# Expert output also kept unsplit in SBUF, activation sums formed there, one more pass by seven products

## The chip, the cores and the metric

The kernel runs on one core of a Trainium2 chip. The metric is the device time of one execution in microseconds (us); several executions are timed and their median is given. One execution more is recorded by the hardware profiler.

The engines are TensorE (PE in the views; PEld is its weight load), VectorE (DVE), ScalarE (ACT), GpSimd (POOL) and SyncE (SP), which issues most DMA transfers. Each works through its own list of instructions in order and waits for the others by semaphores. SBUF is the memory beside the engines, PSUM the memory that TensorE writes.

## The reference

Bucketed attention over 2 x 8 heads of 768 tokens gives x (1536 tokens x 512). A router sends each token to one of 8 experts. Then a gated layer follows, with `d_ff` of 1536:

```
for e in range(E):
    mask = e_idx == e
    h = np.maximum(x[mask] @ w1[e], 0.0)
    out[mask] = gate_w[mask, None] * eom[mask, e, None] * (h @ w2[e])
...
a = x @ w_a
b = x @ w_b
return (a * b @ w_out).astype(np.float32)
```

## The kernel before, in words

**Precision.** Every product is made of three: an operand is split into a rounded high part (suffix `h`, type F32R) and the rest (`l`), and high times high, low times high and high times low are added in PSUM. The high part is a ScalarE copy into F32R, the low part a subtraction on VectorE or GpSimd.

**Stages.** Attention comes first; its program is untouched. Then the expert stage (from about 260 us): 8 experts in 8 steps each. A step multiplies the tokens of an expert by a piece of w1 (`mm1`), takes the result out of PSUM as `hl` (high part on ScalarE, low part on VectorE), and multiplies the `hl` of the step before by a piece of w2 (`mm2`). `y_sum` and `y_store` take an expert's result out in the first two steps of the next expert: `y_store` writes the high part `y_h` on ScalarE and the low part `y_l` on VectorE, at a column that is read from a register (the count of tokens ahead of the expert). `y_evac` does it for the last expert. Tokens are thus columns 0 to 1535 of `y_h` and `y_l`; the four rows of 128 features are the index `d`.

**Second layer** (from 436 us). The columns are two tiles of 768 (`c` = 0 and 1), the 1536 features of the layer are 12 chunks of 128 (`f`). A pass is one chunk for one tile; here it is called f0c0, f0c1, f1c0, f1c1, f2c0 and so on, which is also the order in time. A pass makes a and b for its 768 tokens and multiplies them, in two halves of 384 tokens. There are two ways:

- `ab`: for each half 2 x 4 x 3 products of 384 columns, 48 a pass. The a bank is copied out by ScalarE (L1068), VectorE multiplies it by the b bank (L1069), `rounded` splits the result into `gh` (ScalarE) and `gl` (VectorE, queued after the next half's product).
- `seven`: Strassen's scheme in Winograd's form over two halves of the tokens and two halves of the features, 7 x 2 x 3 = 42 products a pass. It needs sums of weights (`s1` to `s4`, `s_work`) and sums of activations (t1 to t4, `t_work`), both split again. Its first product is copied out as p1 (L1185), the sum u2 adds p1 to the second, and the third adds to the first's bank, so it waits until p1 has been copied; the fourth (`s3`) adds to the second's bank and waits for u2.

Before, f0 and f1 go by `ab` for both tiles, and f2 to f11 by `seven`. The activation sums are made in these four passes from `y_h + y_l` in a buffer `accs`, which later holds the accumulators of 9 of the 12 output blocks (the other three keep a PSUM bank each):

```
t1, t2, t3, t4 = TF = [af[:, o:o + 768].rearrange("p (a b) -> p a b", a=2) for o in at]
...
whole(t3, lo_d, b), whole(t1, lo_d, a), tt(t1, t3, t1), whole(t2, hi_d, b), tt(t3, t2, t3),
tt(t2, t2, t1), tt(t4, yh[:, hi_d, a], t2), tt(t4, t4, yl[:, hi_d, a], ALU.add), hi(1),
```

**Side work.** Between the products stand fill units (`outp`: three matmuls of 512 columns that multiply `gh`, `gl` by the output weights; every second unit is followed by scaling its bank on ScalarE or VectorE) and the conversion of later weights. These arrive as 64-bit floats in pieces of 512 KB (`r2`, loaded by `w2_load` in the order of `SEQ`). A conversion is a chain over two engines: `w2_a` (t, ScalarE), `w2_s` (flags, VectorE), `w2_k` (x, ScalarE, which also issues the next load), `w2_b` (the shift b, VectorE). `w2_c` splits a piece of output weights (h2 on ScalarE, l2 on GpSimd), `part` one of the weights or weight sums into a `pc` (high part on ScalarE, low part on GpSimd). `todo_of` says at which of seven steps of a pass each is issued, `units` which fill units it has, and the loop at the end (L1247 to L1283) emits the passes. The order of every engine is the order in which the code emits.

In the `ab` passes steps 0 to 2 come behind the first half's matmuls and steps 3 to 6 behind the second's; in `seven`, step k comes behind product k.

Of the kernel before, what the change touches and what calls it, by code (L numbers as in the profile page):

```python
# [23 lines left out]
C = 224  # L24
# [9 lines left out]
def attn_moe_kernel(ctx: ExitStack, tc: tile.TileContext, xin, cst, projd, wblk, wmoe, w2in, out):  # L34
# [567 lines left out]
    with tc.manual_schedule():  # L602
# [209 lines left out]
        for y in (y_h, y_l):  # L812
# [4 lines left out]
        s2 = ctx_2.enter_context(tc.tile_pool(name="s2", bufs=3, reuse_waits="tile"))  # L817
# [23 lines left out]
        def w2_a(*k):  # L841
            T2[k] = c2.tile([128, 512], F32, tag="t2", name="t2", bufs=5)
            f64_hi(R2[k], T2[k])

        def w2_s(*k):
            X2[k] = c2.tile([128, 512], U32, tag="x2", name="x2")
            DVE.tensor_scalar(out=X2[k], in0=T2[k].bitcast(U32), scalar1=0x80000000, scalar2=None, op0=ALU.bitwise_and)

        def w2_k(*k):
# [5 lines left out]
            w2_load(SEQ.index(k) + 3)  # L855
# [15 lines left out]
        SW = {}  # L871
# [5 lines left out]

        def part(m, nm):
            src = SW[nm] if nm in SW else a_part(m, nm)
            p = s2.tile([128, 2, 256], F32R, tag="pc", name="pc", bufs=9)  # L880
# [103 lines left out]
        def cc_work():  # L984
# [20 lines left out]
            (7, 7): [ids_load],  # L1005
# [3 lines left out]
        for n, (e, f) in enumerate(steps):  # L1009
# [13 lines left out]
            if e == E - 4 and f in (2, 4, 6):  # L1023
# [19 lines left out]
        accs = fast.tile([128, 9, 512], F32, name="accs")  # L1043
        af = accs.rearrange("p a b -> p (a b)")
# [13 lines left out]
        def ab(c, f, hf):  # L1058
# [8 lines left out]
            a = tmp(("c11", "c21")[hf])  # L1067
# [6 lines left out]
        def outp(k, f):  # L1074
# [36 lines left out]
        def t_work(c):  # L1111
            yh, yl = y_h.bitcast(F32), y_l.bitcast(F32)
            at = ((3072, 0, 768, 1536), (2304, 0, 768, 1536))[c]
            t1, t2, t3, t4 = TF = [af[:, o:o + 768].rearrange("p (a b) -> p a b", a=2) for o in at]

            def whole(o, d, n):
                return lambda: DVE.tensor_tensor(out=o, in0=yh[:, d, n], in1=yl[:, d, n], op=ALU.add)

            def tt(o, x, y, op=ALU.subtract):
                return lambda: DVE.tensor_tensor(out=o, in0=x, in1=y, op=op)  # L1120

            def hi(i):
                return lambda: ACT.activation(TH[c][i], TF[i], ACTF.Copy)

            def low(i):
                th = TH[c][i].bitcast(F32) if i else yh[:, lo_d, n2[c]]
                return lambda: DVE.tensor_tensor(out=TL[c][i], in0=TF[i], in1=th, op=ALU.subtract)

            a, b = n1[c], n2[c]
            return [  # L1130
                whole(t3, lo_d, b), whole(t1, lo_d, a), tt(t1, t3, t1), whole(t2, hi_d, b), tt(t3, t2, t3),
                tt(t2, t2, t1), tt(t4, yh[:, hi_d, a], t2), tt(t4, t4, yl[:, hi_d, a], ALU.add), hi(1),
                hi(2), low(1), hi(3), low(2), low(3),
            ], [hi(0), low(0)]

        def s_work(m, k):
            def new(nm):
                SW[nm] = fast.tile([128, 256], F32, tag=nm, name=nm)
                return SW[nm]

            if k == 0:
                DVE.tensor_tensor(out=new("s1"), in0=a_part(m, "21"), in1=a_part(m, "22"), op=ALU.add)
                DVE.tensor_tensor(out=new("s2"), in0=SW["s1"], in1=a_part(m, "11"), op=ALU.subtract)
            elif k == 1:
                DVE.tensor_tensor(out=new("s3"), in0=a_part(m, "11"), in1=a_part(m, "21"), op=ALU.subtract)
            else:
                DVE.tensor_tensor(out=new("s4"), in0=a_part(m, "12"), in1=SW["s2"], op=ALU.subtract)

# [14 lines left out]
        def seven(c, m, fill, side, low):  # L1163
# [40 lines left out]
            c21 = add(tmp("c21"), y, p1)  # L1204
# [139 lines left out]
```

## Time and profile before

| | |
|---|---|
| median of 3 runs | 741.96 us (741.78 to 743.85) |
| the profiled execution | 742.49 us |
| its span, first to last instruction | 740.7 us |
| mean granted TensorE clock | 0.992 of 2.4 GHz |
| TensorE busy, matmuls | 715.0 us (97%), 4561 |
| VectorE busy | 554.2 us (75%), 1099 instructions |
| ScalarE busy | 439.6 us (59%), 929 |
| GpSimd busy | 223.0 us (30%), 261 |
| bytes moved by DMA | 88.48 MB, mean 119 GB/s |

Matmuls overlap at their ends, so the busy time of TensorE is no measure of how densely they follow each other; the start of one to the start of the next is. An engine that shows no idle time in a stretch may still be late for another. In the rows of the timelines the bracket at the end tells how long the engine had been idle and which instruction, by engine, tile and line, released it. Times in rows are from the span's start. The granted clock is a share of 2.4 GHz; TensorE has two levels, 1.2 and 2.4.

### The profile page before, as it was taken

To read this page: it belongs to the slowest core of one execution; us is meant where nothing else is said; L and a number is where in the kernel's file an instruction comes from. 1 tells how busy PE (TensorE), PEld (TensorE's weight loads), DVE (VectorE), ACT (ScalarE), POOL (GpSimd) and SP (SyncE) were. 2 spreads that over 40 slices of the span, in tenths; PEclk is the share of its full clock that TensorE was granted. 3 is DMA by queue.
4 is the path that set the end of the run, shared out by engine and by line. 5 is a ranking of instruction groups with operands and counts; after the bars stand their busy time and mean duration, and the time that the engine had idled before them with its cause. 6 is when DMAs were issued, how large, how long until landed. Compare 5 with 4: busy or idle time off the path is not lost.

```text
span 740.7 us, 13120 instructions
## 1 busy us (share of the span) xinstructions
PE 715.0 (97%) x4561; PEld 612.0 (83%) x4562; DVE 554.2 (75%) x1099; ACT 439.6 (59%) x929; POOL 223.0 (30%) x261
## 2 busy tenths in 40 slices
PE   8899999999999999999999998799999999999995
PEld 6676777776776789999999997788999999999994
DVE  6778777888776678777778858866777777777653
ACT  6878777777777357666677745456443453434311
POOL 3233232333533283212210002133223332233215
PEclk9999999999999999999999999899999999999998
DMA  7357351321301068888898612121212212120003
GB/s 239 118 214 262 102 167 58 105 69 66 134 8 60 15 223 241 241 188 243 267 238 275 209 30 85 38 78 57 86 35 80 86 58 86 33 81 31 1 30 145
DMA packets 42681, 88.48 MB, mean 119 GB/s; under 512 B 7328, under 2 KB 10736, under 8 KB 42608
## 3 DMA queue, kind: packets, MB, share of 16 engines
q1 hardware_dynamic: 39936, 81.07, 35.5%
q0 software_dynamic: 2304, 6.31, 2.3%
q8 instruction: 38, 0.62, 0.4%
q14 instruction: 35, 0.29, 0.1%
q10 hardware_dynamic: 368, 0.20, 0.1%
HBM read 73.32 MB, written 13.12 MB: 117 GB/s over the span
## 4 chain that ended last, share of the span: by engine, by line
PE 79%; DVE 7%; issue 6%; ACT 3%; POOL 3%; DMA 2%; SPq 0%; POOLq 0%; ACTq 0%; DVEq 0%
PE tp L186 9%; PE av L201 8%; PE y L951 6%; PE s L158 4%; PE s L159 4%; PE h L913 4%; PE h L912 3%; PE h L911 3%; PE y L952 3%; PE aba L1156 3%; PE abb L1156 3%; PE aba L1158 3%; PE aba L1157 3%; PE abb L1158 3%; PE abb L1157 3%
## 5 line engine op out<-in xcount | busy, mean ns | idle before, releaser
L164 DVE TENSOR_REDUCE mm<-s 128x1 f32<-128x768 f32 x96 | 91.1, 949 | 25.1 <-PE s L159 24.1
L173 ACT ACTIVATE p<-s,sb 128x768 f32<-128x768 f32 x96 | 94.8, 988 | 21.7 <-DVE sb L165 21.0
L186 PEld LDWEIGHTS tp<-cs,p 128*128 128x128 f32 x576 | 64.2, 140 | 36.7 <-ACT p L173 23.4
L485 DVE TENSOR_TENSOR wl<-wr,wh 128x512 fp32r<-128x512 f32 x125 | 81.5, 692 | 8.4 <-ACT wh L484 3.1
L186 PE MATMUL tp<-cs,p 128*128 128x128 f32 x576 | 82.2, 279 | 4.8 <-ACT p L173 3.9
L190 ACT ACTIVATE pt<-tp 128x384 f32<-128x384 f32 x143 | 64.9, 487 | 32.6 <-PE tp L186 32.6
L484 ACT ACTIVATE wh<-wr 128x512 fp32r<-128x512 f32 x128 | 73.7, 623 | 3.2 <-DMA wr<-wmoe 3.0
L951 PE MATMUL y<-hl,wh 128*128 128x448 f32 x224 | 74.8, 377 | 0.1
L158 PE MATMUL s<-tk,tq 76*128 76x384 f32 x192 | 73.1, 381 | 0.3 <-DVE tq L135 0.3
L911 PE MATMUL h<-xh,wh 128*128 128x224 f32 x256 | 71.5, 279 | 0.2 <-ACT xh L418 0.2
L913 PE MATMUL h<-xh,wl 128*128 128x224 f32 x256 | 70.7, 276 | 0.2 <-DVE wl L485 0.2
L912 PE MATMUL h<-xl,wh 128*128 128x224 f32 x256 | 70.3, 274 | 0.3 <-DVE xl L419 0.3
L882 POOL TENSOR_TENSOR pc<-t,pc 128x256 fp32r<-128x256 f32 x38 | 30.0, 791 | 128.8 <-ACT pc L881 59.8
L201 PE MATMUL av<-pt,v 128*64 128x384 f32 x360 | 68.0, 499 | 0.2 <-DVE r L225 0.2
L1052 ACT ACTIVATE gh<-c 128x384 fp32r<-128x384 f32 x28 | 14.7, 526 | 88.2 <-DVE c L1175 67.8
L159 PE MATMUL s<-bk,bq 128*128 128x384 f32 x192 | 65.1, 339 | 0.0
L952 PE MATMUL y<-hl,wl 128*128 128x224 f32 x224 | 59.6, 266 | 0.0
L911 PEld LDWEIGHTS h<-xh,wh 128*128 128x128 f32 x256 | 49.0, 191 | 1.3 <-ACT xh L418 0.4
L913 PEld LDWEIGHTS h<-xh,wl 128*128 128x128 f32 x256 | 49.2, 192 | 0.4 <-DVE wl L485 0.4
L912 PEld LDWEIGHTS h<-xl,wh 128*128 128x128 f32 x256 | 49.2, 192 | 0.5 <-DVE xl L419 0.5
L201 PEld LDWEIGHTS av<-pt,v 128*64 128x64 f32 x360 | 21.9, 136 | 32.7 <-issue 24.5
L882 POOL TENSOR_TENSOR pc<-s,pc 128x256 fp32r<-128x256 f32 x40 | 36.0, 910 | 42.8 <-ACT pc L881 42.8
(235 smaller groups left out, 1921.9 us busy)
## 6 DMA issues: line engine op xcount, KB each, us to landing
wr<-wmoe SPq DMA_DIRECT2D x128, 256.0 KB
r<-w2in SPq DMA_DIRECT2D x36, 512.0 KB
x<-xin SPq DMA_DIRECT2D x30, 384.0 KB
xr<-zero SPq DMA_DIRECT2D x13, 512.0 KB
xg<-xr SPq DMA_DIRECT2D x14, 256.0 KB
v<-xin SPq DMA_DIRECT2D x16, 192.0 KB
wb<-wblk SPq DMA_DIRECT2D x1, 640.0 KB
x<-xin SPq DMA_DIRECT2D x3, 192.0 KB
```

The lines of the kernel that those rows point to most:

```text
L158: PE.matmul(p[:, c, :384], T[h, 0][:76, qs], T[h, 1][:76, sl], start=True, stop=False)
L159: PE.matmul(p[:, c, :384], B[h, 0][:, qs], B[h, 1][:, sl], start=False, stop=True)
L164: DVE.tensor_reduce(out=m[:, 1:2], in_=st[g][:, :, :384], axis=AX.XY, op=ALU.min)
L173: ACT.activation(p.rearrange("p (c n) -> p c n", c=2), st.pop(g)[:, :, :384], ACTF.Exp, scale=scl.pop(g), bias=nbs.pop(g), accum_out=sums[ ...
L186: PE.transpose(ps[:, j * 128:(j + 1) * 128], pt_[g][:, k * 128:(k + 1) * 128], ident)
L201: PE.matmul(av[h][c * 64:(c + 1) * 64, :384], v, PT[h][:, k, c * 384:(c + 1) * 384], start=(k == 0), stop=(k == NT - 1), skip_group_check= ...
L485: eng.tensor_tensor(out=l, in0=r, in1=h.bitcast(F32), op=ALU.subtract)
L911: PE.matmul(ps, wh, xh, start=first, stop=False)
L912: PE.matmul(ps, wh, xl, start=False, stop=False)
L913: PE.matmul(ps, wl, xh, start=False, stop=last)
L951: PE.matmul(p, wh[:, w], hl, start=(f == 0), stop=False, skip_group_check=True)
L952: PE.matmul(p[:, 0], wl[:, w], hl[:, 0], start=False, stop=(f == 7), skip_group_check=True)
```

## The change

The expert result is stored a third time, unsplit, as `y_w` (128 x 4 x 1760, F32): `y_store` gets four ScalarE copies more, the last expert two, and `y_w` is cleared by four memsets on GpSimd. `t_work` makes t1 to t4 in place in `y_w`, by four subtractions per tile instead of eight operations. The columns of `y_w` then hold the nine accumulators; `accs` is gone. Pass f1c0 goes by `seven`, f1c1 stays with `ab`. So the sums of tile 0 have to be ready by f1c0, and so have the weight sums of chunk 1, which are new: `s_work(1)` stands in the last two steps of the expert stage, and eight pieces of chunk 1 (the seven of `seven` and 21, which f1c1 needs) instead of four are made in f0c0 and f0c1. The conversion of (2,1) moves from f0c1 to f1c1. To make room, `r2` has 2 buffers instead of 3 (a load is issued two pieces ahead, not three), `t2` 4 instead of 5, `x2` 1 instead of 2; `h2`, `l2` and five of nine `pc` buffers lie in a pool that reuses the expert stage's memory.

The diff, cut (moved but unchanged functions are left out):

```diff
+        y_w = yp.tile([128, 4, N + C], F32, name="y_w")
+        for y in (y_h.bitcast(F32), y_l.bitcast(F32), y_w):
             for d in range(4):
-                POOL.memset(y.bitcast(F32)[:, d], 0.0)
-        r2 = ctx_2.enter_context(tc.tile_pool(name="r2", bufs=3, reuse_waits="tile"))
+                POOL.memset(y[:, d], 0.0)
+        r2 = ctx_2.enter_context(tc.tile_pool(name="r2", bufs=2, reuse_waits="tile"))
...
-        SEQ = [(0, 0), (0, 1), (1, 0), (1, 1), (0, 2)]
-        for m in range(2, 12):
+        SEQ = [(0, 0), (0, 1), (1, 0), (1, 1), (0, 2), (2, 0), (1, 2), (2, 1)]
+        for m in range(3, 12):
...
-            w2_load(SEQ.index(k) + 3)
+            w2_load(SEQ.index(k) + 2)
...
+        def pc_tile(shape, dt, nm):
+            pcs[0] += 1
+            return (s2 if (pcs[0] - 1) % 9 < 4 else fast).tile(shape, dt, tag="pc", name=nm, bufs=4 if (pcs[0] - 1) % 9 < 4 else 5)
...
         def y_store(e):
             sl = bass.ds(o_regs[e], C)
             for d in range(4):
-                y = YS.pop((e, d))
+                y = YS[e, d]
                 ACT.activation(y_h[:, d, sl], y, ACTF.Copy)
                 DVE.tensor_tensor(out=y_l[:, d, sl], in0=y, in1=y_h.bitcast(F32)[:, d, sl], op=ALU.subtract)
+            for d in range(4):
+                ACT.activation(y_w[:, d, sl], YS.pop((e, d)), ACTF.Copy)
...
+            (7, 6): [lambda: s_work(1, 0)],
+            (7, 7): [ids_load, lambda: s_work(1, 1), lambda: s_work(1, 2)],
...
-            if e == E - 4 and f in (2, 4, 6):
+            if e == E - 4 and f in (2, 4):
                 w2_load(f // 2 - 1)
...
         for i in range(2):
             y_evac(E - 1, i)
+        for i in range(2):
+            src = Y[E - 1][i].rearrange("p (a b) -> p a b", a=2)[:, :, :C]
+            ACT.activation(y_w[:, 2 * i:2 * i + 2, bass.ds(o_regs[E - 1], C)], src, ACTF.Copy)
...
-            o = accs[:, (k - 6) % 9]
+            if not own:
+                d, at = AT[k - 3]
+                o = y_w[:, d, at:at + 512]
...
+            a, b = n1[c], n2[c]
+            w = (y_w[:, lo_d, a], y_w[:, hi_d, b], y_w[:, lo_d, b], y_w[:, hi_d, a])
...
+                tt(w[0], w[2], w[0]), tt(w[2], w[1], w[2]), tt(w[1], w[1], w[0]), tt(w[3], w[3], w[1])
+            ] + [g(i) for i in (1, 2, 3, 0) for g in (hi, low)]
...
+            if (c, f) == (0, 0):
+                for k, g in zip((0, 0, 0, 1, 3, 3, 4, 5, 6, 6), t):
+                    m[k].append(g)
+                conv(0, 2, 1, 1, 1, 2)
+                put(4, w2_c, 0)
+                for k, nm in ((2, "11"), (3, "s2"), (4, "12"), (5, "s3"), (6, "s1")):
+                    put(k, part, 1, nm)
+            elif (c, f) == (1, 0):
+                t = t_work(0)
+                put(0, t[10])
+                put(1, t[11])
+                conv(2, 0, 2, 2, 2, 3)
+                put(4, cc_work)
+                for k, nm in ((4, "22"), (5, "s4"), (6, "21")):
+                    put(k, part, 1, nm)
+            elif (c, f) == (0, 1):
+                t = t_work(1)
+                for k in range(4):
+                    put(k, t[k])
+                conv(1, 2, 3, 4, 4, 5)
+                put(6, w2_c, 1)
+            elif (c, f) == (1, 1):
+                conv(2, 1, 0, 0, 0, 1)
+                for k, g in zip((1, 1, 2, 3, 3, 4), t[4:10]):
+                    m[k].append(g)
+                for k in range(3):
+                    put(2 + k // 2, s_work, 2, k)
+                conv(3, 0, 4, 4, 4, 5)
+                conv(3, 1, 5, 5, 5, 6)
+                for k, nm in ((0, "11"), (1, "12"), (2, "s2"), (3, "s3"), (3, "s1"), (4, "22"), (5, "s4")):
+                    put(k, part, 2, nm)
+                put(6, t[10])
+                put(6, t[11])
...
-                if f < 2:
+                if f < 2 and (c or not f):
                     for hf in range(2):
+                        if (c, f, hf) == (0, 0, 0):
+                            for g in work[0]:
+                                g()
+                            work[0] = []
                         last, low = low, ab(c, f, hf)
```

How the order moves, at two places. VectorE, from the first product c of f0c0 on (c_6176 before; the first and second half's product are c_6176 and c_6219), before:

```order
L1069 TENSOR_TENSOR c_6176<-abb,c_6176 128x384
L1117 TENSOR_TENSOR accs<-y_h,y_l 128x768
L847 TENSOR_SCALAR x_6185<-t_6182 128x512
L1117 TENSOR_TENSOR accs<-y_h,y_l 128x768
L859 SCALAR_TENSOR_TENSOR t_6182<-t_6182,x_6185 128x512
L1120 TENSOR_TENSOR accs<-accs 128x768
L1069 TENSOR_TENSOR c_6219<-abb,c_6219 128x384
L1054 TENSOR_TENSOR gl<-c_6176,gh 128x384
L1117 TENSOR_TENSOR accs<-y_h,y_l 128x768
L1120 TENSOR_TENSOR accs<-accs 128x768 x2
L1120 TENSOR_TENSOR accs<-y_h,accs 128x768
```

and now, where the second half's product writes p_6263 and the shifted weights are t_6226:

```order
L1142 TENSOR_TENSOR y_w<-y_w 128x2x384 x3
L1093 TENSOR_TENSOR c_6219<-abb,c_6219 128x384
L1142 TENSOR_TENSOR y_w<-y_w 128x2x384
L848 TENSOR_SCALAR x_6228<-t_6226 128x512
L860 SCALAR_TENSOR_TENSOR t_6226<-t_6226,x_6228 128x512
L1093 TENSOR_TENSOR p_6263<-abb,p_6263 128x384
L1078 TENSOR_TENSOR gl<-c_6219,gh 128x384
L1142 TENSOR_TENSOR tl_6184<-y_w,th_6178 128x768
L1142 TENSOR_TENSOR tl_6185<-y_w,th_6179 128x768
L1142 TENSOR_TENSOR tl_6186<-y_w,th_6180 128x768
```

Three of the four sums stand ahead of the first product, the additions of y_h and y_l are gone, and the three low parts of tile 0 stand in the second half of f0c0.

ScalarE in f1c1, from the split of the second half's product (c_6536, `gh`) to the copy p1 of f2c0 (p_6587); q are the banks that are scaled into the accumulators, t and x the conversion, before:

```order
L1052 ACTIVATE gh<-c_6536 128x384
L1096 ACTIVATE accs<-q_6499,cc 128x512
L850 ACTIVATE x_6547<-r_6326 128x512
L881 ACTIVATE pc<-s_6434 128x256
L881 ACTIVATE pc<-s_6430 128x256
L1123 ACTIVATE th_6143<-accs 128x768
L1096 ACTIVATE accs<-q_6556,cc 128x512
L881 ACTIVATE pc<-t_6284 128x256
L881 ACTIVATE pc<-s_6437 128x256
L1123 ACTIVATE y_h<-accs 128x2x384
L1185 ACTIVATE p_6587<-aba 128x384
```

and now, where the split and one scaled bank stand ahead of these rows, and p_6631 is p1:

```order
L1145 ACTIVATE th_6183<-y_w 128x768
L900 ACTIVATE pc<-s_6538 128x256
L900 ACTIVATE pc<-s_6534 128x256
L496 ACTIVATE t_6595<-r_6442 128x512
L851 ACTIVATE x_6597<-r_6442 128x512
L900 ACTIVATE pc<-t_6509 128x256
L1122 ACTIVATE y_w<-q_6590,cc 128x512
L496 ACTIVATE t_6610<-r_6514 128x512
L851 ACTIVATE x_6612<-r_6514 128x512
L900 ACTIVATE pc<-s_6582 128x256
L1145 ACTIVATE y_h<-y_w 128x2x384
L1191 ACTIVATE p_6631<-abb 128x384
```

Two conversions (t_6595 and t_6610, each with its x) stand behind the third high part, where there was none; the third, of (2,1), stands further ahead in the same pass, as the two of before do (the x of the second is in the rows).

## Rows read from the trace of the kernel before

**Rows 1.** TensorE timeline 452 to 496: start us, us, engine, line, operation, [idle before <- releaser].
```profile
457.29 0.45 PE L911 MATMUL aba<-y_h,pc 128*128 128x384 f32 x1 [3.06 <-ACT c L1068]
...
477.29 0.79 PE L1087 MATMUL q<-h,gl 128*128 128x512 f32 x1 [3.78 <-DVE gl L1054]
...
491.57 0.44 PE L1156 MATMUL aba<-y_h,pc 128*128 128x384 f32 x1 [0.57 <-ACT p L1185]
...
494.50 0.44 PE L1156 MATMUL abb<-th,pc 128*128 128x384 f32 x1 [0.92 <-DVE u L1171]
```

**Rows 2.** Windows: stretch, us, busy of PE, PEld, DVE, ACT, POOL, granted clock, DMA share, GB/s.
```profile
473.50:476.60 3.10, 0.01 (x1) 0.00 (x0) 3.07 (x5) 0.00 (x0) 0.00 (x0) 0.99 0.01 3
476.60:483.40 6.80, 6.11 (x18) 5.73 (x19) 2.54 (x5) 5.49 (x11) 2.49 (x3) 0.50 0.25 78
```

**Rows 3.** TensorE timeline, 483.7 to 485.5; eight matmuls are left out.
```profile
483.70 0.34 PE L911 MATMUL abb<-y_h,pc 128*128 128x384 f32 x1
...
485.27 0.39 PE L1085 MATMUL q<-h,gh 128*128 128x512 f32 x1
485.50 0.40 PE L1086 MATMUL q<-l,gh 128*128 128x512 f32 x1
```

**Rows 4.** VectorE and GpSimd timelines of pass f1c1.
```profile
475.35 0.95 DVE L1127 TENSOR_TENSOR y_l<-accs,y_h 128x768 fp32r<-128x768 f32 x1
476.22 0.55 DVE L1069 TENSOR_TENSOR c<-abb,c 128x384 f32<-128x384 f32 x1
...
478.02 0.42 DVE L847 TENSOR_SCALAR x<-t 128x512 uint32<-128x512 uint32 x1
...
490.06 1.49 DVE L1127 TENSOR_TENSOR tl<-accs,th 128x768 fp32r<-128x768 f32 x1
...
481.53 0.74 POOL L882 TENSOR_TENSOR pc<-t,pc 128x256 fp32r<-128x256 f32 x1 [0.61 <-PE aba L913]
```

**Rows 5.** Expert stage: ScalarE and TensorE timelines around 331 and 421.
```profile
330.90 1.22 ACT L975 ACTIVATE y_h<-yt 128x224 f32 x4
332.28 0.36 ACT L924 ACTIVATE hl<-h 128x224 fp32r<-128x224 f32 x1 [0.16 <-PE h L913]
...
334.63 0.38 PE L951 MATMUL y<-hl,wh 128*128 128x448 f32 x1
...
420.93 0.33 ACT L924 ACTIVATE hl<-h 128x224 fp32r<-128x224 f32 x1
...
422.01 0.27 PE L940 MATMUL y<-hl,wh 128*128 128x224 f32 x1
422.27 0.37 PE L943 MATMUL y<-hl,wh 128*128 128x224 f32 x1
```

**Rows 6.** Windows, as group 2: the 2.2 us in which one 512 KB load moves.
```profile
507.40:509.60 2.20, 2.20 (x13) 2.06 (x13) 1.41 (x3) 1.70 (x4) 1.35 (x2) 1.00 0.75 235
```

**Rows 7.** TensorE and VectorE timelines at the end of f0c0.
```profile
444.86 0.34 PE L911 MATMUL aba<-y_h,pc 128*128 128x384 f32 x1
...
445.39 0.55 DVE L1069 TENSOR_TENSOR c<-abb,c 128x384 f32<-128x384 f32 x1
```

**Rows 8.** ScalarE timeline of pass f1c1, one row of each kind.
```profile
476.81 0.52 ACT L1052 ACTIVATE gh<-c 128x384 fp32r<-128x384 f32 x1 [5.81 <-DVE c L1069]
477.24 0.67 ACT L496 ACTIVATE t<-r 128x512 f32<-128x512 f32 x1
477.80 0.41 ACT L881 ACTIVATE pc<-t 128x256 fp32r<-128x256 f32 x1
478.18 0.69 ACT L1096 ACTIVATE accs<-q,cc 128x512 f32<-128x512 f32 x1
478.77 0.77 ACT L850 ACTIVATE x<-r 128x512 uint8<-128x512 uint8 x1
...
479.70 0.83 ACT L1123 ACTIVATE th<-accs 128x768 fp32r<-128x768 f32 x1
...
491.03 0.48 ACT L1185 ACTIVATE p<-aba 128x384 f32<-128x384 f32 x1
```

More of the change, by code (lines that the diff above doesn't have):

```diff
@@ L876, in a_part, with s_work, new @@
             return T2[m, i][:, o:o + 256]
+        def s_work(m, k):
+            def new(nm):
+                SW[nm] = s2.tile([128, 256], F32, tag=nm, name=nm, bufs=1)
+                return SW[nm]
+            if k == 0:
+                DVE.tensor_tensor(out=new("s1"), in0=a_part(m, "21"), in1=a_part(m, "22"), op=ALU.add)
+                DVE.tensor_tensor(out=new("s2"), in0=SW["s1"], in1=a_part(m, "11"), op=ALU.subtract)
+            elif k == 1:
+                DVE.tensor_tensor(out=new("s3"), in0=a_part(m, "11"), in1=a_part(m, "21"), op=ALU.subtract)
+            else:
+                DVE.tensor_tensor(out=new("s4"), in0=a_part(m, "12"), in1=SW["s2"], op=ALU.subtract)
         def part(m, nm):
             src = SW[nm] if nm in SW else a_part(m, nm)
-            p = s2.tile([128, 2, 256], F32R, tag="pc", name="pc", bufs=9)
+            p = pc_tile([128, 2, 256], F32R, "pc")
             ACT.activation(p[:, 0], src, ACTF.Copy)
@@ L1041, in attn_moe_kernel @@
         G = {}
-        accs = fast.tile([128, 9, 512], F32, name="accs")
-        af = accs.rearrange("p a b -> p (a b)")
+        AT = ((0, 0), (1, 0), (2, 0), (3, 0), (2, 1024), (3, 1024), (0, 1024), (1, 1024), (2, 512))
         def tmp(nm):
@@ L1129, in t_work @@
-            a, b = n1[c], n2[c]
+                th = TH[c][i].bitcast(F32) if i else y_h.bitcast(F32)[:, lo_d, b]
+                return tt(TL[c][i], w[i], th)
             return [
[L1131 to L1147, printed above, removed]
+                tt(w[0], w[2], w[0]), tt(w[2], w[1], w[2]), tt(w[1], w[1], w[0]), tt(w[3], w[3], w[1])
+            ] + [g(i) for i in (1, 2, 3, 0) for g in (hi, low)]
@@ L1228, in todo_of, with conv, put @@
-            if c == 0:
-                m[3].append(lambda: w2_c(f))
+            m = [[] for _ in range(7)]
+            def conv(n, i, *at):
+                for k, g in zip(at, (w2_a, w2_s, w2_k, w2_b)):
+                    m[k].append(lambda g=g: g(n, i))
+            def put(k, g, *a):
+                m[k].append(lambda: g(*a))
+            if f < 2:
+                t = t_work(c)
+            if (c, f) == (0, 0):
[31 more added lines that the diff above has]
+                put(6, t[11])
+            elif c == 0:
+                conv(f, 2, 0, 1, 1, 2)
+                put(3, w2_c, f)
+                if f < 11:
+                    for k, at in ((0, 4), (1, 4), (2, 5)):
+                        put(at, s_work, f + 1, k)
@@ L1230, in todo_of @@
             elif f < 11:
-                for k, nm in enumerate(ORDER if f else ("11", "12", "21", "22")):
-                    m[k].append(lambda nm=nm: part(f + 1, nm))
+                for i in range(2 * (f < 10)):
+                    conv(f + 2, i, *((0, 1, 1, 2), (3, 4, 4, 5))[i])
+                for k, nm in enumerate(ORDER):
+                    put(k, part, f + 1, nm)
             return m
@@ L1242, in units @@
             return [(k, i) for k in range(3) for i in (f - 2, f - 1) if i >= 0]
-        ts = [t_work(c) for c in range(2)]
-        todo = ts[0][0] + ts[1][0]
         low = None
```

51 lines of the change are left out of this document (12 added, 39 removed).

## Prediction

> **What bounds the kernel now.** TensorE is busy for 97% of the span, so I looked first for the stretch where it isn't. The view by slices sends the reader to 450 to 500 us, the first passes of the second layer; TensorE's own timeline there shows who is waited for [rows 1]. Pass f1c0 starts 3.06 late because ScalarE had not copied the half ahead of it out of PSUM; the fill matmuls of f1c1 stand still for 3.78 behind a VectorE subtraction; f2c0 waits 0.57 for the copy p1 and 0.92 for the sum u2. The windows show a second price of the 3.78: work stopped at 473.5, the granted clock went from 0.99 to 0.50 at 476.6, that is from 2.4 to 1.2 GHz, and stayed there for 6.8 us [rows 2]. 6.1 us of that were under work, so about 3 us were lost (2.8 by the matmuls in it). The 3.06 wait left no such mark. After 494.5 TensorE streams matmuls to the end, so a gain before that point reaches the end whole, through the last products and the row scatters behind them.
>
> So the sum is a race over one stretch, from the first product of f0c0, near 436, to 494.50 (product s3 of f2c0). All times below are on the clock of the profiled execution: 742.49 us, of which 740.7 are the span; the median of the runs, 741.96, is 0.53 lower.
>
> **What leaves.** A matmul of 384 columns costs TensorE 0.175 (nine from 483.70 to 485.27), one of 512 columns 0.23 [rows 3]. f1c0 by seven products has 42 instead of 48: 1.05 us less. The sums t1 to t4 lose per tile three additions of high and low part and one more operation: 8 VectorE operations of 0.87 each (475.35 to 476.22 [rows 4]), 7 us, all from this stretch.
>
> **What is added in the expert stage.** Each of seven y_store calls gets four ScalarE copies of 224 columns. The y_h copies beside them take 1.22 for four [rows 5]; back to back that is 1.2 more. Behind them stands the copy hl of the next step. For most experts the start of hl then goes from 332.28 to 333.3; with its 0.36 and VectorE's 0.4 behind it, it is done by 334.1, and the matmul that reads it comes at 334.63: free. For the last stored expert it isn't: hl moves from 420.93 to 422.15, the matmuls reading it stand at 422.01 and 422.27 [rows 5], and the second needs VectorE's 0.4 behind hl's end at 422.45. Cost **0.6**, once. The two copies of the last expert run under the first product, which reads y_h only: nothing. The four memsets on POOL follow eight others and end before its next work; the s_work of chunk 1 takes VectorE's idle time in the last steps: nothing. If that idle time were not there, its four operations (0.34 to 0.42 each) would hold hl by 1.5 us.
>
> **Buffers and loads.** The accumulators move from accs into y_w with the same operations: nothing. With four t2 buffers a t in later passes waits for GpSimd's piece 12 of the step before, which is done in 0.74 plus a meeting, while a step is 1.75 of TensorE (six matmuls and a unit): nothing, and ScalarE would hold it up by half a us at most where that fails. With two buffers each load is issued one piece later. The tightest is (2,2): issued after w2_k of (3,0), read four microseconds later by the schedule below. One load moves in 2.2 us at 235 GB/s [rows 6]; the price lies between nothing and the 1 us by which a late landing could hold ScalarE. I take nothing, as 1.8 us are over.
>
> **The chain through the passes.** f0c0 starts as before and TensorE goes over to f0c1 at 444.86; the product c of its second half runs on VectorE from 445.39 to 445.94 [rows 7]. VectorE's three first sums wait for the last y_w copy (two of 0.6 behind y_h, near 437.8) and take 2.6, so they are through when the first half's product needs VectorE, a half of TensorE (24 x 0.175 = 4.2) ahead of that one. From there ScalarE decides. Its operations follow each other 0.1 closer than they last [rows 8]: gh 0.42, t 0.57, pc 0.31, scaled q 0.59, flags x 0.67, th 0.73, copy out of PSUM 0.48 in full; h2 I take at 0.52, between pc and t.
>
> - f0c1, second half. Its bank is free when ScalarE has copied the half before; ahead of that copy stand gh, three th, h2 and four pc, 4.4 us, from 445.5 on (b on VectorE ends a little sooner than the sum that stood there). The copy ends at 450.4, TensorE is done at 448.9 or 449.0: **1.5** late.
> - f1c0. VectorE ends that half's product at 451.6, behind three low parts and two meetings with GpSimd (below). ScalarE then has gh, a th and a t, to 453.3; VectorE's fourth low part runs to 454.2, the flags to 454.6; x and the copy end at 455.8, TensorE is ready at 454.6: **1.2**. The 3.06 of before becomes this.
> - f1c1. f1c0 takes 42 x 0.175 and three fill units of 0.7, to 465.3, and the first bank of f1c1 is the one that f1c0's last sum reads. The sum's last matmuls end at 465.6, but VectorE is in the shift b (512 columns, some 0.6 by the 0.87 for 768) and a low part until 466.6, and the sum takes 0.55: 467.1, **1.8** late, a new wait, with every matmul queued behind it.
> - f2c0. f1c1 takes 48 x 0.175, six units of 0.7 and 0.1 of waiting: 479.8. Two products and two units later, at 483.3, TensorE needs its bank copied (p1).
>
> p1 is the last of a long ScalarE queue, as the order of f1c1 shows: from the first gh (472.2) there are 2 gh, 3 t, 3 x, 7 pc, 3 q, 4 th and one copy, 11.8 us, and waits for VectorE: 0.57 for each flag round (0.42 and the ends of two operations), 1.3 for s_work, which has to convert (2,1) first, 0.7 for the second half's product, 0.2 for a low part: 3.9. Before, the same pass had one conversion less (1.24 and its round). So p1 starts at 487.9 and ends at 488.3: TensorE stands **5.0** us, the longest wait of all. u2 comes at 489.9, s3 needs it at 490.1: no wait. With the 0.6, s3 starts at 490.7 instead of 494.50: **3.8 gained**.
>
> **The clock.** 5.0 us of rest are more than the 3.78 that took the clock down. If it falls as it did, 3.1 us after work stops (486.4), and stays for 6.8 (to 493.2), then 4.9 us are under work and cost half, **2.4**. Bounds: nothing (as after 3.06) and the 2.8 paid before. I take 2.4. Sum: 742.49 - 3.8 + 2.4 = 741.1; as a median 0.53 less, **740.6**.
>
> **GpSimd beside VectorE.** f1c0 as seven products, with f1c1 as it was, needs eight pieces for chunk 1, not four, so the stretch has 15 GpSimd pieces where it had 11. A VectorE operation of 768 that meets one lasts 1.49 instead of 0.95, 0.54 more, while the GpSimd piece alone lasts 0.74 [rows 4]. I put in 0.54 for each meeting (1.06 for the 512-column l2). The Trainium skill (SBUF — State Buffer, Who interferes with whom) says that a GpSimd operation and a VectorE one with two SBUF inputs lock each other out for the whole instruction. The trace agrees that they exclude each other, but not on the length. By that rule the sum is the rival below.
>
> **Rivals.** A change of 0.3% (2.2 us) is about what a measurement of this kernel can tell from none.
>
> 1. *Forecast*, 0.34: p1 is late by 4 to 6 us and the clock falls: 740.6.
> 2. *The clock holds*, 0.24. For it: one wait of 3.06 left it up, and nothing in the rows says when exactly it falls. Against: 5.0 is longer than the wait that took it down. Then 742.49 - 3.8 - 0.53 = 738.2.
> 3. *The queues overlap better*, 0.19. My schedule puts every meeting with GpSimd on the path and lets ScalarE wait for each. If the chain to p1 is 2 us shorter, the wait is 3.0, the clock stays, and 5.8 are gained: 736.2; without any p1 wait 733. Against: 11.8 of the 15.7 us are plain ScalarE work.
> 4. *Whole lock*, 0.07. With 0.74 for each meeting, and 1.3 for each l2, the same chain gives p1 at 490.2, 5.4 us late; the gain is 1.6, u2's 0.92 in it, and 2.3 go to the clock: 743.2, as a median 742.6.
> 5. *Slower*, 0.16: the y_w copies have a moving place in y_w, and if each takes 0.6, twice a y_h copy, hl is late for every stored expert, not one: 1.2 us more per call, of which 0.6 are over at the six others. That adds 6 x 0.6 and 1.2 at the seventh: 745.4 as a median. It decides from 0.45 per copy on. For it: nothing in the trace writes y_w; against: y_h has the same kind of address at 0.30.
>
> That the seven-product pass doesn't do what it says is excluded by the order: TensorE has 6 matmuls fewer.
>
> **Numbers.** Faster is 2 and 3 (0.43), within 0.3% is 1 and 4 (0.41), slower 5 (0.16). The likeliest case alone spans 739 to 742.5 (2.8 to 0.5 for the clock, 1 us either way for p1). The range reaches from 734.5, in the middle of case 3 (733 to 736.2), to 744.0, short of case 5's centre; over half of case 5 and half of case 3 are outside, 0.2 together.
>
> **What would show it.** Right: the 3.78 gone; a wait of TensorE of 4 to 6 us early in f2c0, released by the ScalarE copy p1, and a clock of 0.50 behind it; three waits of 1 to 2 us in f0c1, f1c0 and f1c1; s3 of f2c0 at 490.7, 3.8 sooner than now, and 1.4 of that left where the clock has come back up; one wait of about 0.6 at 422. Wrong: no long wait for p1, so that the stretch ends 6 us or more earlier; waits for hl at every expert; or a landing load that ScalarE's t waits for.

## Result, and the profile after

| | before | changed |
|---|---|---|
| median | 741.9 us (741.78 to 743.85, 4 runs) | 752.16 us (751.40 to 752.80, 4 runs) |
| the profiled execution | 742.49 us | 752.34 us |
| its span | 740.7 us | 750.5 us |

The changed kernel is slower: the ratio is 1.0132, with a 95% interval of 1.0112 to 1.0151. The forecast was 740.6, in a range from 734.5 to 744.0. The head of the page of the changed kernel:

```profile
span 750.5 us, 13177 instructions
...
PE 715.7 (95%) x4555; PEld 610.3 (81%) x4556; DVE 555.3 (74%) x1100; ACT 449.2 (60%) x963; POOL 231.2 (31%) x269
```

TensorE is as busy as before (715.0 then), so the 9.8 us are waits. The two spans are compared at three instants that both programs have:

- First matmul of the expert stage: 259.73 before, 261.43 now. These 1.70 are no part of the change: in this execution the constants `cs`, issued at 7.2 in both, landed later, TensorE stood for 2.57 until 13.97, and the granted clock was 0.66 from 15 to 20 us. Two of the eleven experiments that start from the changed kernel show the same (e2 with 1.86, e8 with 2.42, the clock at 0.50 behind both); over all eleven this matmul comes between 259.24 and 261.22. So it is the execution and not the program.
- From there to the first wait of f0c0: 176.80 before, 177.36 now. How long the first steps wait for weights differs between executions; from the last transposes of tokens to f0c0's first matmul it was 26.42 before and 27.02 now, 0.60 more, with one wait for `hl` (0.27, at 424.09).
- From that wait to s3 of f2c0: 57.97 before, 57.78 now. **The stretch that the prediction is about gave 0.2.**
- From s3 to the end: 246.20 before, 253.93 now. **7.7 us were lost where the prediction saw nothing.**

Without the 1.70 the profiles are 8.1 apart, and the medians 10.3. What the executions without a profile lost besides is not shown.

What TensorE waited for, in the view of waits (engine, matmul, releaser: us in total, times, longest), first the stretch 420 to 510, then 500 to 740 of the changed kernel:

```profile
PE abb L1162 <- ACT p L1191: 6.7, 1, 6.7
PE aba L930 <- DVE u L1177: 1.7, 1, 1.7
PE aba L930 <- ACT c L1092: 1.4, 1, 1.4
PE aba L1162 <- ACT p L1092: 0.9, 1, 0.9
PE y L959 <- ACT hl L943: 0.3, 1, 0.3
...
PE aba L1162 <- DVE u L1177: 5.9, 7, 0.9
```

The first four answer to [rows 1]: the 3.06 and the 3.78 are gone, three waits of 0.9 to 1.7 and one long wait for p1 stand in their place. The last line is new: seven waits of 0.85 for a sum `u`, one behind each pair of passes from f3 to f9. The first of them in TensorE's timeline:

```profile
540.04 0.39 PE L1111 MATMUL q<-h,gl 128*128 128x512 f32 x1
541.28 0.44 PE L1162 MATMUL aba<-th,pc 128*128 128x384 f32 x1 [0.85 <-DVE u L1177]
541.56 0.34 PE L1163 MATMUL aba<-tl,pc 128*128 128x384 f32 x1
```

From the first start to the second these are 1.24; a matmul of 512 columns takes 0.23 [rows 3]. Each wait costs 1.01, seven cost 7.1. The matmul behind each comes 0.1 late as well (0.28 instead of 0.175 from start to start), which is about the rest of the 7.7.

VectorE ahead of it, at the end of pass f3c1 of the changed kernel, and the GpSimd piece and the split of that time:

```profile
536.96 0.56 DVE L1177 TENSOR_TENSOR p<-abb,p 128x384 f32<-128x384 f32 x1 [0.84 <-PE abb L1164]
537.55 0.92 DVE L1181 TENSOR_TENSOR p<-c,p 128x384 f32<-128x384 f32 x1
538.40 0.74 DVE L1124 SCALAR_TENSOR_TENSOR y_w<-q,cc,y_w 128x512 f32<-128x512 f32 x1
539.06 0.68 DVE L860 SCALAR_TENSOR_TENSOR t<-t,x 128x512 uint32<-128x512 uint32 x1
539.66 1.09 DVE L1078 TENSOR_TENSOR gl<-p,gh 128x384 fp32r<-128x384 f32 x1
540.68 0.55 DVE L1177 TENSOR_TENSOR u<-aba,u 128x384 f32<-128x384 f32 x1
...
538.51 0.53 ACT L1076 ACTIVATE gh<-p 128x384 fp32r<-128x384 f32 x1 [1.32 <-DVE p L1181]
...
539.49 0.85 POOL L901 TENSOR_TENSOR pc<-t,pc 128x256 fp32r<-128x256 f32 x1 [1.42 <-ACT pc L900]
```

And the same sums in the kernel before, with the matmul that needs the last one's bank:

```profile
534.73 0.56 DVE L1171 TENSOR_TENSOR c<-aba,p 128x384 f32<-128x384 f32 x1
535.33 0.99 DVE L1175 TENSOR_TENSOR c<-c,c 128x384 f32<-128x384 f32 x1
536.24 0.74 DVE L1098 SCALAR_TENSOR_TENSOR accs<-q,cc,accs 128x512 f32<-128x512 f32 x1
536.91 0.56 DVE L1054 TENSOR_TENSOR gl<-c,gh 128x384 fp32r<-128x384 f32 x1
537.38 0.55 DVE L1171 TENSOR_TENSOR u<-abb,u 128x384 f32<-128x384 f32 x1
...
538.04 0.39 PE L1156 MATMUL abb<-th,pc 128*128 128x384 f32 x1
```

Now the shift b of the second conversion (539.06) stands between the scaling and gl. It takes 0.6 and pushes gl behind the start of a GpSimd piece; gl then lasts 1.09 instead of 0.56, and the pass's last sum ends 4.3 after the sum that begins the chain, not 3.2. The second product of the next pass needs the bank that this sum reads. The change had moved the second conversion of f2c1 to f9c1 one step later, in lines that my cut of the diff did not show:

```diff
-                m[2 * k].append(lambda a=(n, i): w2_a(*a))
+                for i in range(2 * (f < 10)):
+                    conv(f + 2, i, *((0, 1, 1, 2), (3, 4, 4, 5))[i])
```

Before, the second stood at steps 2, 3, 3 and 4.

The long wait, in ScalarE's and VectorE's timelines of the changed kernel:

```profile
490.09 0.83 ACT L1145 ACTIVATE y_h<-y_w 128x768 fp32r<-128x768 f32 x1
492.68 0.49 ACT L1191 ACTIVATE p<-abb 128x384 f32<-128x384 f32 x1 [1.77 <-DVE gl L1078]
...
490.95 1.17 DVE L1142 TENSOR_TENSOR y_l<-y_w,y_h 128x768 fp32r<-128x768 f32 x1 [0.23 <-ACT y_h L1145]
492.04 0.55 DVE L1078 TENSOR_TENSOR gl<-p,gh 128x384 fp32r<-128x384 f32 x1
```

ScalarE is through its queue at 490.92 and then stands for 1.77. The copy p1 waits for gl, not for the product: its output buffer `p1` is also the one in which f1c1 made its second half's product (`tmp(("c11", "p1")[hf])`, which was `"c21"`), and gl still has to read it.

The clock fell in that wait as forecast (windows: us, busy of PE, PEld, DVE, ACT, POOL, granted clock, DMA share, GB/s):

```profile
489.40:493.20 3.80, 0.00 (x0) 0.00 (x0) 2.33 (x3) 2.03 (x5) 1.04 (x1) 0.54 0.63 208
493.20:496.60 3.40, 3.38 (x10) 3.10 (x11) 1.68 (x3) 2.30 (x4) 0.00 (x0) 0.51 0.19 33
496.60:500.00 3.40, 3.40 (x19) 3.17 (x18) 0.96 (x2) 1.21 (x2) 0.17 (x1) 1.00 0.31 122
```

The nine matmuls from 493.22 to 496.57 took 3.35 instead of 1.74 (six of 0.175, three of 0.23), 1.6 lost, against 2.4 forecast. The wait was longer than forecast, so less of the low clock fell under work.

### The profile page after: what moved, and what is told of

It reads as the page before. It is cut to its first block, busy times and chain, and to the rows that moved or that the text cites. A ratio compares the mean times of both kernels' runs of the same rounds, so it can differ in the third digit from the quotient of the medians.

```text
span 750.5 us, 13177 instructions
## 1 busy us (share of the span) xinstructions
PE 715.7 (95%) x4555; PEld 610.3 (81%) x4556; DVE 555.3 (74%) x1100; ACT 449.2 (60%) x963; POOL 231.2 (31%) x269
## 5 line engine op out<-in xcount | busy, mean ns | idle before, releaser
L901 POOL TENSOR_TENSOR pc<-t,pc 128x256 fp32r<-128x256 f32 x38 | 32.1, 848 | 152.0 <-ACT pc L900 80.4
L1076 ACT ACTIVATE gh<-p 128x384 fp32r<-128x384 f32 x24 | 12.6, 525 | 67.2 <-DVE p L1181 64.7
L851 ACT ACTIVATE x<-r 128x512 uint8<-128x512 uint8 x36 | 28.4, 790 | 37.7 <-DVE x L848 37.7
```

What stands on the lines that cost most here:

```text
L901: POOL.tensor_tensor(out=p[:, 1], in0=src, in1=p.bitcast(F32)[:, 0], op=ALU.subtract)
```

## The experiments

Times beside the kernel before on the same chips, whose medians there were 743.2 to 743.7 (741.6 to 745.8); the changed kernel was timed on the first chip only, so its copies with one edit are compared with 752.16 by their traces as well.

| kernel | median us (range, runs) | ratio to before, 95% |
|---|---|---|
| e1_conv_early | 745.46 (744.33 to 746.77, 10) | 1.0028, 1.0016 to 1.0040 |
| e2_own_buffer | 750.13 (749.10 to 750.94, 4) | 1.0089, 1.0069 to 1.0108 |
| e3_before_conv_late | 751.25 (750.34 to 751.94, 4) | 1.0106, 1.0087 to 1.0125 |
| e4_no_yw_in_store | 750.62 (1 run) | |
| e5_three_edits | 745.49 (744.16 to 746.28, 10) | 1.0027, 1.0014 to 1.0039 |
| e6_one_conv_out | 741.38 (739.86 to 743.02, 10) | 0.9971, 0.9957 to 0.9986 |
| e7_two_convs_out | 739.81 (738.39 to 740.66, 8) | 0.9949, 0.9933 to 0.9964 |
| e8_f1c0_ab | 751.34 (750.73 to 752.96, 4) | 1.0101, 1.0074 to 1.0128 |
| e9_sums_later | 739.58 (738.67 to 740.43, 5) | 0.9947, 0.9925 to 0.9969 |
| e10_acts_later | 738.42 (737.63 to 740.06, 4) | 0.9932, 0.9905 to 0.9959 |
| e12_bank_order | 740.54 (740.26 to 742.76, 5) | 0.9961, 0.9946 to 0.9976 |
| e11_all | 735.92 (734.94 to 736.69, 5) | 0.9894, 0.9878 to 0.9910 |

### The place of the shift, taken away and added

```diff
-                    conv(f + 2, i, *((0, 1, 1, 2), (3, 4, 4, 5))[i])
+                    conv(f + 2, i, *((0, 1, 1, 2), (2, 3, 3, 4))[i])
```

> The changed kernel, with one edit: in the passes f2c1 to f9c1 the second conversion is put back to steps 2, 3, 3, 4 (the change had moved it to 3, 4, 4, 5). Theory A, the place of the shift b: at step 5 it stands on VectorE between the scaling and gl, so the pass's last sum and the next pass's second product are late by 1.01 (0.85 of idle time and 0.16 of restart), seven times. Then the seven waits of 0.85 for u vanish, 7.1 us go, and the time is about 745.0. Theory B, the buffers: the waits come from two r2, four t2 or one x2 buffer, or from the GpSimd pieces in the reused pool. Then at least 0.5 of each wait stays and the time is 748.5 to 752.2. Theory C, the meeting alone: gl lasts 1.09 instead of 0.56 because it meets a GpSimd piece; if it still does so without b, 0.3 to 0.5 of each wait stays: 747 to 749.

Measured 745.46, 6.7 below the changed kernel. None of the seven waits of 0.85 is left. From s3 to the end its trace has 248.2 instead of 253.9; 1.2 of these are the low clock, which lasted 2.3 us beyond s3 in this execution. VectorE in the same place, and the GpSimd piece:

```profile
538.47 0.74 DVE L1124 SCALAR_TENSOR_TENSOR y_w<-q,cc,y_w 128x512 f32<-128x512 f32 x1
539.13 0.56 DVE L1078 TENSOR_TENSOR gl<-p,gh 128x384 fp32r<-128x384 f32 x1
539.61 0.55 DVE L1177 TENSOR_TENSOR u<-aba,u 128x384 f32<-128x384 f32 x1
...
539.55 0.74 POOL L901 TENSOR_TENSOR pc<-t,pc 128x256 fp32r<-128x256 f32 x1 [1.42 <-ACT pc L900]
```

The buffers and the pools are those of the changed kernel, so theory B falls. gl lasts 0.56 again, since it now starts 0.42 ahead of the piece, so nothing stays of C either. But b and the meeting went together: no run parts b's 0.6 from the 0.5 of the meeting that it brings about. The other way round, in the kernel before:

```diff
-                m[2 * k].append(lambda a=(n, i): w2_a(*a))
+                o = 2 * k + (k == 1 and c == 1 and f >= 2)
+                m[o].append(lambda a=(n, i): w2_a(*a))
```

(the other three parts follow at `o + 1` and `o + 2`).

> The kernel before, with one edit: in the passes f2c1 to f9c1 the second conversion goes from steps 2, 3, 3, 4 to 3, 4, 4, 5, as the change has it; all buffers stay as they are in the kernel before. Theory A (the place of b alone): seven or eight waits of about 0.85 for u appear at the second product of the passes behind, and the time is 748 to 750. Theory B (the buffers of the change): no such waits, 741.9 within 0.5. Theory C (the meeting with GpSimd decides): waits of 0.3 to 0.5, 744 to 746.

Measured 751.25, 7.6 above the kernel before. Its waits from 500 to 740:

```profile
PE abb L1156 <- DVE u L1171: 6.0, 7, 0.9
```

The one step alone makes the kernel before nearly as slow as the changed one, and taking it out of the changed one gives back 6.7. It is shown in both directions.

### The buffer of p1

```diff
-            a = tmp(("c11", "p1")[hf])
+            a = tmp(("c11", "u3")[hf])
```

> The changed kernel, with one edit: the second half's product of an ab pass is written into the buffer u3, which no instruction uses there, instead of p1's. Theory A: the copy p1 of f2c0 starts 1.77 late because its buffer is read until gl of f1c1 is done; then it starts when ScalarE ends y_h, the wait of 6.69 becomes 4.9, and the time is 750.4 if the clock falls as before. Theory B: p1 would be late anyhow, since something else holds ScalarE there: within 0.3 of 752.2, and the wait stays above 6.4.

Measured 750.13. The wait in TensorE's timeline:

```profile
490.58 0.69 PE L1162 MATMUL abb<-y_h,pc 128*128 128x384 f32 x1 [4.82 <-ACT p L1191]
```

4.82 instead of 6.69, and 55.93 instead of 57.78 from f0c0's first wait to s3: theory A. What is left is the queue that the prediction counted.

### The copies of y_w

> The changed kernel without the four ScalarE copies of y_w in each of the seven y_store calls; the activation sums are then formed from a y_w that is zero outside the last expert's columns. Theory A (one late hl, at the seventh call): f0c0's first wait comes 0.5 to 0.6 sooner after the first matmul of the expert stage, and the one wait for hl at 424 goes. Theory B (a cost at each of the seven calls): 1 us or more sooner. Nothing in the later passes changes: seven waits of 0.85.

The edit takes the two lines of the copies out of `y_store`. From the last transposes to f0c0's first matmul it took 26.43, 0.60 less than in the changed kernel, and the wait at 424 was gone. From the stage's first matmul to f0c0's first wait it was 176.19 instead of 177.36; what is over 0.60 there lies in the first steps, whose wait for weights made it 176.80 in the kernel before and 176.18 in e3, the same program up to there. So A, at one call; the 1.17 would meet B's number, but no matmul waits for `hl` at the other stored experts. A copy into y_w costs what one into y_h does, as ScalarE's timeline of the changed kernel says:

```profile
421.46 1.22 ACT L994 ACTIVATE y_h<-yt 128x224 f32 x4
422.58 1.22 ACT L997 ACTIVATE y_w<-yt 128x224 f32 x4
```

### f1c0 by ab again

`f < 2` takes the place of `f < 2 and (c or not f)`, `s_work(1)` and the pieces s1 to s4 of chunk 1 go (four, where the expectation says three), and the split of t1 for tile 0 goes to f1c1. There it reads columns of y_w that hold accumulators by then, so later products get other numbers.

> The changed kernel with f1c0 by the ab way again: no weight sums and no three pieces for chunk 1, and the split of t1 for tile 0 moves behind f1c0, into f1c1. Theory A (the seven-product pass saves its six matmuls and the three pieces cost nothing): 1.0 slower by the matmuls, and ScalarE's queue to p1 grows by the 0.74 of the split: 753.9. Theory B (the fuller GpSimd and ScalarE queue of f0c0 and f0c1 costs more than the six matmuls give): 751 or less, with the waits of 1.39 and 0.88 in f0c1 and f1c0 smaller.

Measured 751.34, which cannot be told from 752.16 (from f0c0's first wait to s3 57.44, against 57.78). Neither theory's number, but B's direction: the waits in f0c1, ahead of f1c0 and ahead of f1c1 fell from 1.39, 0.88 and 1.68 to 0.77, nothing and nothing, 3.2 together. Against that stand 1.05 for six more matmuls, 0.6 more for p1 (7.28), 0.86 for a GpSimd `l2` and 0.25 for a piece. So the pass by seven products gave nothing here that can be told: its sums and pieces cost about what its six matmuls save.

### The waits of the stretch

> The changed kernel with the edits of e1_conv_early and e2_own_buffer, and the conversion of (1,2) in f1c0 at steps 2, 3, 3, 4 instead of 3, 4, 4, 5. Theory A (a shift b at step 5 makes the pass's last sum late, in f1c0 as in the later passes): the wait of 1.68 ahead of f1c1 goes, the wait for p1 stays at 4.8, and the time is 745.5 - 2.0 - 1.8 = 741.7. Theory B (ScalarE's queue in f1c1 sets p1's time whatever comes before): the 1.68 go to the wait for p1, which becomes 6.5, and the time is 743.5.

```diff
-                conv(1, 2, 3, 4, 4, 5)
+                conv(1, 2, 2, 3, 3, 4)
```

e5 measured 745.49: both fell. The wait ahead of f1c1 grew, to 2.50, with the clock at 0.54 behind it (468 to 470), and another of 0.22 stood ahead of it; the wait for p1 stayed at 4.82. A step earlier, b waited 0.45 for ScalarE's flags and held up the sums behind it. So a later place of b is not what sets this wait.

> As e5_three_edits, and the conversion of (3,1) and the split of t1 for tile 1 (y_h, y_l) move from f1c1 to f2c0, with (2,2) behind (3,1). Theory A (the wait for p1 is the length of ScalarE's queue): the queue loses 0.74 + 1.24 and a flag round of 0.5, so the wait goes from 4.8 to 2.3; if the clock then holds, its 1.6 to 2.1 come back too: 737.0 to 737.5, else 739.3. Theory B (VectorE or GpSimd hold the queue up, or the moved work makes new waits in f2c0): the wait for p1 stays above 3.5, or u waits of 1 us and more come up in f2c0: 739.5 to 742.

e6 measured 741.38, 4.1 below e5:

```profile
490.60 0.44 PE L1162 MATMUL abb<-y_h,pc 128*128 128x384 f32 x1 [2.31 <-ACT p L1191]
```

The wait for p1 became 2.31, as A says of the queue, though the clock fell behind it too (0.59 from 492 to 496). The time is in B's range, but neither of B's signs came: the 2.50 of e5 were in this kernel as well.

> As e6_one_conv_out, and the conversion of (3,0) moves to f2c0 too; there the order is (3,0), (3,1), (2,2), and the output weights (2,2) are split in f2c1. Theory A: another 1.24 + 0.5 leave the queue, the wait for p1 is 0.6 or less, the clock stays at 0.99 throughout, and the time is 735 to 736. Theory B: VectorE's longer queue in f2c0 makes its sums late, as b at step 5 did: waits for u of 1 to 2 us in f2c0 and f2c1, 737 to 739.

e7 measured 739.81:

```profile
487.42 0.45 PE L1162 MATMUL abb<-y_h,pc 128*128 128x384 f32 x1 [0.29 <-ACT p L1191]
```

The wait for p1 is 0.29, so the queue explains it. Of B, one wait came: 0.98 in f2c0, where weight sums of chunk 3 stand ahead of a sum. The time is above both theories', since the wait ahead of f1c1 (2.48) and the clock behind it are in this kernel too.

> As e7_two_convs_out, but the conversion of (1,2) is back at steps 3, 4, 4, 5 of f1c0, and the four subtractions for tile 1 (3.7 us of VectorE) move from f1c0 to the time of f1c1's first half, where VectorE waits for the first product. Theory A (f1c0's last sum is late because VectorE's queue is full in that pass, not because of the place of b): the waits of 0.22 and 2.48 go, the clock stays at 0.99 behind them (2 us), and the time is 735 to 735.5, with the wait for p1 under 0.5. Theory B (b at step 5 is what is late there as in the later passes): a wait of 0.8 or more ahead of f1c1 stays. Theory C (the moved subtractions hold up f1c1's first product or the queue to p1): the wait for p1 grows to 2 or more, 737 to 739.

e9 measured 739.58: with four subtractions fewer on VectorE in f1c0, the wait ahead of f1c1 is still 1.80, so theory A fell. The moved subtractions made a wait of 2.88 for gl in f1c1, though not for p1, as C had it. The 1.80 are B's sign, but not by B's cause. Its VectorE and ScalarE rows show what is left, the first sum behind f1c0's sixth product up to its last sum, and TensorE:

```profile
465.70 0.56 DVE L1177 TENSOR_TENSOR p<-abb,p 128x384 f32<-128x384 f32 x1
466.29 0.56 DVE L1181 TENSOR_TENSOR p<-c,p 128x384 f32<-128x384 f32 x1
466.77 0.68 DVE L860 SCALAR_TENSOR_TENSOR t<-t,x 128x512 uint32<-128x512 uint32 x1
467.44 0.56 DVE L1078 TENSOR_TENSOR gl<-p,gh 128x384 fp32r<-128x384 f32 x1
467.91 0.55 DVE L1177 TENSOR_TENSOR u<-aba,u 128x384 f32<-128x384 f32 x1
...
466.88 0.52 ACT L1076 ACTIVATE gh<-p 128x384 fp32r<-128x384 f32 x1 [0.50 <-DVE p L1181]
...
466.38 0.34 PE L1164 MATMUL aba<-y_h,pc 128*128 128x384 f32 x1
468.52 0.45 PE L930 MATMUL aba<-y_h,pc 128*128 128x384 f32 x1 [1.80 <-DVE u L1177]
```

gl cannot start before 467.40, since gh ends there; b, which ends at 467.45, stands in that gap. The last sum is queued behind gl, 2.8 after the chain begins, while TensorE has six matmuls of 0.175 and no fill unit, and then needs the very bank that the sum reads. In the later passes a unit, the last product, the next pass's first product and another unit follow the sixth, 3.5 us; in the kernel before the last sum was through at 537.93 and the matmul that needs its bank came at 538.04. There the chain just fitted, until 1.1 were added.

> As e9_sums_later, and the split of t4 for tile 0 goes from f0c0 to steps 2 and 3 of f1c0, the conversion of (2,0) from f0c1 to f1c0. Theory A (the waits of 1.39 in f0c1 and 0.91 ahead of f1c0 are the length of ScalarE's and VectorE's queues): 0.74 and 1.24 less of ScalarE, and the 1.39 becomes 0.3 to 0.6, the 0.91 goes: 733.5 to 734. Theory B (the moved work fills VectorE's queue in f1c0 again): a wait of 1 us or more ahead of f1c1 comes back: 735 or more.

e10 measured 738.42. The 1.39 became 0.65 and the 0.91 went, as A says; the 1.80 and the 2.88 of e9 stayed, so the time is not A's.

> The changed kernel with the edits of e1_conv_early and e2_own_buffer, and in f1c1 the a products use the bank abb and the b products aba (not the other way round); the conversion of (1,2) stays at steps 3, 4, 4, 5. Theory A (the 1.68 ahead of f1c1 are a chain with nothing to cover it: f1c0 has no fill unit behind its sixth product, and sum, product, split on ScalarE, gl and the last sum follow each other, 2.8 us, against 1.05 of TensorE; the first matmuls of f1c1 need the bank that the last sum reads): with the other bank first, 2.1 us of matmuls cover it, the wait goes, the wait for p1 stays at 4.8, and the time is 1.7 below the sum of e1 and e2 (743.4): 741.7. Theory B (ScalarE's queue sets p1 whatever comes before): the 1.7 go to the wait for p1, 743.4. Theory C (VectorE's queue of sums for tile 1 sets it): a wait of over 1 us stays ahead of f1c1 or within its first half.

```diff
-            p = [pa.tile([128, 512], F32, tag="ab" + "ab"[i], name="ab" + "ab"[i]) for i in range(2)]
+            tags = ("abb", "aba") if (c, f) == (1, 1) else ("aba", "abb")
+            p = [pa.tile([128, 512], F32, tag=tags[i], name=tags[i]) for i in range(2)]
```

e12 measured 740.54, 1.2 below what A expected. TensorE goes from f1c0 to f1c1 without a wait and waits for p1 only at 489.15:

```profile
467.51 0.34 PE L1165 MATMUL aba<-y_h,pc 128*128 128x384 f32 x1
467.69 0.34 PE L930 MATMUL abb<-y_h,pc 128*128 128x384 f32 x1
...
489.15 0.69 PE L1163 MATMUL abb<-y_h,pc 128*128 128x384 f32 x1 [4.93 <-ACT p L1192]
```

The wait for p1 is 4.93 and did not take the 1.7 over. So it was the chain, and with three edits (the step, the buffer, the bank) the change is faster than the kernel before, 0.9961 (0.9946 to 0.9976).

> As e10_acts_later, with the bank order of e12_bank_order; of the four subtractions for tile 1 two are back in f1c0, one stands ahead of f1c1's first product and one behind its first half; in f2c0 the weight sums of chunk 3 and the flags of (2,2) come behind the last sum. Theory A: the waits of 1.80 (ahead of f1c1), 2.88 (gl, behind four subtractions) and 1.18 (f2c0's sum behind weight sums) go, with 1.5 of clock: 738.4 - 7 = 731 to 732. Theory B: each moved operation makes a wait of its own somewhere else in the stretch, above all gl behind the one subtraction (0.5 to 1) and u2 of f2c1 behind the weight sums: 733 to 736.

Against e10, cut:

```diff
+                put(0, t[2])
+                put(2, t[3])
...
-                    conv(2, 2, 4, 4, 5, 6)
+                    conv(2, 2, 5, 6, 6)
...
+                    put(0, w2_b, 2, 2)
+                    put(1, w2_c, 2)
```

e11 measured 735.92, 1.1% below the kernel before: the best of all, in B's range. The 1.80 and the 1.18 are gone; gl still stands behind one subtraction and a flag round:

```profile
PE q L1112 <- DVE gl L1078: 2.3, 1, 2.3
PE aba L930 <- ACT c L1093: 0.7, 1, 0.7
```

With two further waits taken away it would be nearer to A; that was not tried.

## Why the prediction was wrong

**The step that failed** is in the first part: "After 494.5 TensorE streams matmuls to the end, so a gain before that point reaches the end whole". It is true of the kernel before, but for one wait of 0.25 at 503, and I took it for the changed one, though the change moves a conversion in eight of the later passes; behind seven of them the wait stands. I costed what the change does up to f2c0 and, of the rest, only the buffers. The moved step was worth 7.1 us by the waits, 6.7 and 7.6 by e1 and e3, some two thirds of the loss; without it the time is 745.46, still outside the range. The rival on the other side named the copies into y_w; these took 0.30 each, as in the forecast, and that rival did not occur.

**The second failure** is the sentence "The accumulators move from accs into y_w with the same operations: nothing", which stood for all the renamed buffers. The product of the second half had lost its own buffer to p1's: 1.77 of waiting, and 1.85 less from f0c0's first wait to s3 in e2's trace. That the loads cost nothing held: from 436 us on no ScalarE instruction of the changed kernel waits for one.

**The terms**, forecast and measured:

| term | forecast | measured |
|---|---|---|
| expert stage | 0.6 | 0.60 |
| wait in f0c1 | 1.5 | 1.39 |
| wait ahead of f1c0 | 1.2 | 0.88 |
| wait ahead of f1c1 | 1.8 | 1.68 |
| wait for p1 | 5.0 | 6.69; 4.82 with a buffer of its own |
| clock behind it | 2.4 | 1.6; 2.5 in e2, where the wait is 4.82 |
| later passes | 0 | 7.1 by the seven waits, 7.7 from s3 to the end |

So the race of queues was right within about 0.3 a wait. From f0c0's first wait to s3 the forecast is 53.57, with the clock 55.97; measured were 57.78. The 1.8 between are the buffer's 1.77, 1.0 by which TensorE reached the wait later than I had it, and the clock's 0.8 the other way. On the cause of the wait ahead of f1c1 I was only half right: the bank and the last sum were (e12), but I had the sum wait for VectorE's own queue alone, b and a low part; what holds gl, ahead of the sum, is gh on ScalarE, which ends as late as b does (e9). In this part it is luck that the 1.8 came out.

By the whole-lock rival, GpSimd would stop VectorE for 0.74 and more at each meeting. gl, met by a piece at 539.49, lasted 0.53 longer, near the 0.54 that I put in. This is less than a piece because the piece had begun 0.17 earlier: had gl been held until the piece's end at 540.34 and then taken its own 0.56, it would have ended at 540.90; it ended at 540.75. By the Trainium skill (SBUF — State Buffer, SBUF: two separate sides) the two lock each other out for a whole instruction; this meeting agrees with that but for 0.15. So the rival's price was too high for a meeting that is under way, and the lock itself is not refuted.

## What to carry to other kernels

Where a loop is rescheduled, go through every pass that the diff reaches, not only the stretch with the waits: compare the order of each engine at the end of one pass of each kind, and measure the slack there in the trace of before. In these passes the sum ended 0.1 ahead of need, so one operation of 0.6 between a split and the last sum, with the meeting of 0.5 that it brought about, cost 1.0 us in seven of eight pairs. A buffer's new name is a new wait: ask who reads it last, and on which queue that reader stands.

## What was not expected of the hardware

Behind waits of about the same length the granted clock sometimes fell and sometimes held. The wait of 3.06 left it at 1.00 in the profile of before [rows 1]; the same wait in e3, the same program up to there, took it to 0.50. The window from 456 to 462 (columns as above), before and in e3:

```profile
456.00:462.00 6.00, 4.71 (x26) 4.51 (x27) 4.67 (x7) 3.92 (x8) 1.78 (x2) 1.00 0.40 126
456.00:462.00 6.00, 5.56 (x17) 5.56 (x18) 5.20 (x7) 3.18 (x7) 1.14 (x2) 0.50 0.33 105
```

Behind 2.26 (e11), 2.31 (e6), 2.48 (e7), 2.50 (e5) and 2.88 (e9) it fell too, behind 1.68 and 1.80 it did not. Nor did it stay down equally long: behind the wait for p1 of 6.7 it was at 0.50 for 6.8 us in the changed kernel and for 10.2 in e1, where 5.7 of them were under work and cost 2.7. The times of the kernel before fit this: of its 54 runs beside the experiments, the 20 with a mean clock of 0.991 or more have a median of 742.2, the other 34 one of 744.0; that the 3.06 parts them is not shown, since none of these 54 has a profile here.

I had only the 3.06 to go by and gave "the clock holds" a chance of 0.24 for 5.0. The experiments that shortened a wait to 2 or 3 us still paid the clock's part.
